# A retention and mixture-of-experts kernel: the first expert is chosen earlier, its register is read further back, low weight parts come in threes, and blocks of token rows are turned whole

## The chip, the cores and the metric

The kernel runs on one core of a Trainium2 chip. The core has five engines that run side by side, each with a queue of instructions that it works off in order: TensorE (PE in the profile, with its weight loads as PEld), VectorE (DVE), ScalarE (ACT), GpSimd (POOL) and SyncE (SP), which does little but issue transfers. A transfer can be issued from any queue; here SP loads inputs and weights, ACT stores token rows, and POOL fetches and stores rows by index. Engines wait for one another and for transfers by semaphores. The metric is the device time of one execution in microseconds (us).

## What is computed

A retention layer (attention without softmax, with a decay per head) makes 4608 token rows of 512 numbers. Each row with a positive skip score goes to the one of eight experts with the largest gate logit; the expert is two matrix products with a ReLU between them, and its result, times the gate's probability, is added to the row.

```python
scores = scale * np.matmul(q, k.transpose(0, 1, 3, 2))      # 8 x 8 heads, 576 x 576
Dmat = np.where(rel >= 0, gamma[:, None, None] ** rel[None, :, :], 0.0)
x = np.matmul(scores * Dmat, v)                             # as rows: 4608 x 512
...
do_compute = x @ w_skip > 0
e_idx = np.argmax(xc @ w_gate, axis=1)
gate_w = probs[np.arange(len(xc)), e_idx]
...
h = np.maximum(xc[mask] @ w1[e], 0.0)                       # 512 -> 1024
y[mask] = gate_w[mask, None] * (h @ w2[e])                  # 1024 -> 512
out[do_compute] = xc + y
```

## The kernel before

The program has two stages. In the **retention stage** a loop over g = 0 to 35 makes 128 token rows an iteration. The inputs of an iteration are one tile `u` of 1 MB, loaded from SP in two halves of 512 KB (`load_half`, L430-446) into five rotating buffers: the first half (queries and keys) can be issued when the tile of five iterations before has been read, the second (values and keys by row) is issued one iteration later, behind a block of products. In iteration g,

- GpSimd scales the keys of iteration g + 1 (`keys`, two instructions on L513, written `kn`). TensorE's state products of iteration g + 1 read them, and GpSimd reads the second half of `u`;
- TensorE interleaves the state products of chunk 2g (`ps_s`, L531) with the scores of the next iteration (`psc`, L479), then makes the values of iteration g - 1 (`pxt`, L560), then the second such pair of blocks, then turns the rows of iteration g - 2 (`px`, L584, in `stage_c`);
- ScalarE copies the running state back (L542) and stores token rows; VectorE applies the decays (L495) and evicts the values (L573).

**Gates.** Every fourth iteration logits are made (`pl`, `pn`), `route_a` turns them into masks on VectorE with one exponential on ScalarE (L155), and what is left of the routing stands in a list `todo`, from which `routing` takes a few entries an iteration: `route_b` (ranks of tokens in their experts), one `slots` entry for each group of 128 tokens (VectorE compares ranks to slot numbers, L228, tile `r`; TensorE adds the result to `ps_m`, L233, at the next call), and, after the first 24 groups, `choose_first`. That one counts the tokens of each expert so far, takes the largest as the first expert, and writes its number to `lead_id` (L261). `expert_reg` has SP load this number into a register, since every weight load takes its address from it. `close_first`, after 28 groups, makes the indices of the first expert's rows (`gi`, L295), which GpSimd fetches (L303).

**Weights.** Once the register is there, `weights()` is called at the end of each iteration. In call n it loads weight chunk n (512 KB, L130), and it splits chunk n - 2: ScalarE rounds it to a high part (L643), and GpSimd subtracts that from the chunk in four pieces, the low part (L648). Five chunks are split so in this stage.

In the **expert stage** TensorE runs through the eight experts. Rows of an expert are fetched in blocks of 128, 128 and what is left (`blocks`: for 368, 344, 332, 308, 304, 286, 278 and 276 slots that is 112, 88, 76, 52, 48, 30, 22 and 20 rows). `turn` transposes them 128 columns at a time, block by block (`pt`, L804), before the products of L387.

TensorE's queue is in the order in which the code is written (`manual_schedule`); on the other engines a scheduler orders the instructions by its own estimates, except that those given to `keep_in_program_order` keep their order among themselves. A pool's buffers rotate, and a writer waits for the last reader of its buffer.

In the list below, group 2 of the gates (`KONE`) is the one behind which the first expert is chosen, and its logits are routed in iteration 26.

```python
            if k == KONE:
                todo.append((True, 0, lambda: choose_first(ps_m, cnt)))
                todo.append((False, 0, lambda: regs.append(expert_reg(lead_id[0:1, 0:1]))))
```

An entry whose first field is True is only taken as the first of a call; the number is the iteration from which on it may be taken.

## Time and profile before

| what | us |
|---|---|
| median of 3 runs | 438.65 |
| the three runs | 432.28, 438.65, 443.81 |
| the profiled execution | 432.73 |
| its span, first to last instruction | 431.0 |
| TensorE busy in the span | 391.7 (91%) |
| VectorE, ScalarE, GpSimd busy | 276.3, 186.9, 160.4 |

The profile is of one execution that took 432.73 us, near the lower end of the runs. The page puts the span into 40 equal slices, one digit each, the busy share in tenths:

```profile
span 431.0 us, 13306 instructions
PE   7788988899988589999999999999999999999990
DVE  2595598488589978848755554865654755656430
POOL 4665564545555397150330042033141250400302
PEclk9899999999999989999999999999999999999996
DMA  8899989899986977255673455455465465642101
```

The slices are 10.8 us wide and counted from 0. Up to about 170 us (slice 15) is the retention stage: TensorE at eight or nine tenths, the transfers near full. From about 190 us on TensorE is full and the transfers are half used. Between them the first expert's products overlap with the last gates. In slice 13 TensorE falls to five tenths, and PEclk, the clock granted to it, falls in the slice behind.

### The profile page before, as it was taken

What the parts mean: (1) busy time and instruction counts of PE and PEld (TensorE: products, weight loads), DVE (VectorE), ACT (ScalarE), POOL (GpSimd) and SP (SyncE); (2) the same over time, 40 slices, a digit from 0 to 9 for tenths busy, and PEclk for the clock granted to TensorE, in tenths of its full rate; (3) what the DMA queues carried; (4) which work ended last, traced back from release to release, by engine and by line L of the source; (5) the groups of instructions that cost most, each with busy time, mean ns of one, the idle gap of its engine ahead of it and who ended that gap; (6) DMA issues with size and microseconds to landing.
All of it is one profiled execution on the core that took longest, in us unless ns stands there. A gap on an engine that the chain in (4) does not pass through costs nothing. (4 is left out here: it accounts for less than half of the span.)

```text
span 431.0 us, 13306 instructions
## 1 busy us (share of the span) xinstructions
PE 391.7 (91%) x5482; PEld 351.7 (82%) x5484; DVE 276.3 (64%) x562; ACT 186.9 (43%) x360; POOL 160.4 (37%) x182
## 2 busy tenths in 40 slices
PE   7788988899988589999999999999999999999990
PEld 3576776677777467888999999999999999999980
DVE  2595598488589978848755554865654755656430
ACT  2255444454644457117444434444444445445210
POOL 4665564545555397150330042033141250400302
PEclk9899999999999989999999999999999999999996
DMA  8899989899986977255673455455465465642101
GB/s 311 301 326 314 344 304 314 313 327 307 365 310 232 338 284 240 98 149 207 203 230 117 146 172 193 147 173 185 150 212 172 162 207 173 200 144 77 52 0 52
DMA packets 29023, 92.14 MB, mean 214 GB/s; under 512 B 4119, under 2 KB 4247, under 8 KB 28960
## 3 DMA queue, kind: packets, MB, share of 16 engines
q1 hardware_dynamic: 19584, 71.31, 48.4%
q0 software_dynamic: 3616, 9.86, 6.7%
q10 hardware_dynamic: 5760, 10.09, 6.3%
q8 instruction: 44, 0.72, 0.7%
q14 instruction: 19, 0.16, 0.1%
HBM read 77.07 MB, written 14.55 MB: 213 GB/s over the span
## 5 line engine op out<-in xcount | busy, mean ns | idle before, releaser
L140 DVE TENSOR_TENSOR wlo_w<-w,whi_w 128x1024 fp32r<-128x1024 f32 x59 | 71.9, 1223 | 61.9 <-ACT whi_w L139 61.8
L513 POOL TENSOR_TENSOR kn<-u,tt_sb 64x512 f32<-64x512 f32 x72 | 77.3, 1073 | 67.2 <-PE psc L479 44.2
L843 POOL DMA_INDIRECT out<-rs,sidx x24 | 32.8, 1366 | 156.4 <-DVE rs L842 153.2
L139 ACT CAST whi_w<-w 128x1024 fp32r<-128x1024 f32 x59 | 61.6, 1051 | 61.5 <-PE py L387 59.4
L542 ACT COPY u<-ps_s 64x256 f32<-64x256 f32 x128 | 47.0, 367 | 65.6 <-issue 26.7
L387 PE MATMUL py<-hhi,whi_w 128*128 128x344 f32 (+6 forms) x224 | 70.6, 315 | 0.0
L387 PE MATMUL ph<-xhi,whi_w 128*128 128x344 f32 (+6 forms) x224 | 68.9, 308 | 0.0
L387 PE MATMUL py<-hhi,wlo_w 128*128 128x344 f32 (+6 forms) x224 | 67.8, 303 | 0.0
L387 PE MATMUL ph<-xhi,wlo_w 128*128 128x344 f32 (+6 forms) x224 | 67.8, 302 | 0.0
L387 PE MATMUL ph<-xlo,whi_w 128*128 128x344 f32 (+6 forms) x224 | 67.7, 302 | 0.0
L387 PE MATMUL py<-hlo,whi_w 128*128 128x344 f32 (+6 forms) x224 | 67.6, 302 | 0.0
L531 PE MATMUL ps_s<-u,kn 64*64 64x64 f32 x1024 | 48.8, 227 | 14.4 <-issue 6.4
L531 PEld LDWEIGHTS ps_s<-u,kn 64*64 64x64 f32 x1024 | 39.2, 135 | 26.8 <-issue 10.8
L495 DVE TENSOR_TENSOR u<-psc,dt_sb 64x512 f32<-64x512 f32 x72 | 49.6, 689 | 14.2 <-PE psc L479 8.9
L395 ACT ACTIVATE hhi<-ph 128x344 fp32r<-128x344 f32 (+8 forms) x61 | 26.0, 427 | 64.1 <-PE ph L387 57.0
L479 PE MATMUL psc<-u 64*64 64x64 f32 x1152 | 51.8, 227 | 1.9 <-DVE u L495 0.6
L560 PE MATMUL pxt<-u 128*64 128x64 f32 x1152 | 45.1, 231 | 3.2 <-issue 2.8
L479 PEld LDWEIGHTS psc<-u 64*64 64x64 f32 x1152 | 41.7, 136 | 5.3 <-issue 2.4
L560 PEld LDWEIGHTS pxt<-u 128*64 128x64 f32 x1152 | 39.1, 142 | 7.5 <-issue 4.6
L387 PEld LDWEIGHTS py<-hhi,whi_w 128*128 128x128 f32 x224 | 42.2, 188 | 0.9
L387 PEld LDWEIGHTS ph<-xhi,whi_w 128*128 128x128 f32 x224 | 42.3, 189 | 0.1
L387 PEld LDWEIGHTS ph<-xlo,whi_w 128*128 128x128 f32 x224 | 42.3, 189 | 0.1
(178 smaller groups left out, 645.0 us busy)
## 6 DMA issues: line engine op xcount, KB each, us to landing
u<-qkv SPq DMA_DIRECT2D x72, 512.0 KB, 5.2
w<-w SPq DMA_DIRECT2D x64, 512.0 KB, 3.7
out<-xn ACTq DMA_DIRECT2D x36, 256.0 KB, 5.4
out<-rs,sidx POOLq DMA_INDIRECT x24
xg<-out,gidx POOLq DMA_INDIRECT x21
dt_sb<-dtab ACTq DMA_DIRECT2D x1, 256.0 KB
gt_sb<-dtab ACTq DMA_DIRECT2D x1, 256.0 KB
wg_sb<-wg ACTq DMA_DIRECT2D x1, 64.0 KB, 8.8
```

The source lines that it names most:

```text
L139: nc.scalar.copy(hi, t)
L140: nc.vector.tensor_tensor(lo, t, hi.bitcast(F32), ALU.subtract)
L387: nc.tensor.matmul(ps, x, y, start=first and n == 0, stop=last and n == 3 * len(terms) - 1)
L395: nc.scalar.activation(hi, ph, AF.Relu)
L479: nc.tensor.matmul(psc_t[g][halves[j], c, a, :], u[halves[j], 1 - j, c, a, :], u[halves[j], j, c, a, :], start=c == 0 and a == 0, stop=c = ...
L495: nc.vector.tensor_tensor(u_t[g][h, j], psc[halves[j]], dt_sb[h, c0 : c0 + 2], ALU.mult)
L513: nc.gpsimd.tensor_tensor(kn_t[g][h], u_t[g][h, 2 + j], tt_sb[h, 0, c0 : c0 + 2, :].unsqueeze(3).broadcast_to([D, 2, NPR, D]), ALU.mult,)
L531: nc.tensor.matmul(ps_s[halves[j], a, :], kn_t[g][h, c, a, :], u_t[g][h, 3 - j, c, a, :], start=n % NQ == 0 and a == 0, stop=a == NPR - 1, ...
L542: nc.scalar.copy(u_t[g][halves[j], 3 - j, c], ps_s[halves[j]])
L560: nc.tensor.matmul(pxt[halves[j], a, c * D : (c + 1) * D], u_t[g][:, 3 - j, c, a, :], u_t[g][:, j, c, a, :], start=c == 0 and a == 0, stop ...
L843: put = nc.gpsimd.indirect_dma_start(out=out, out_offset=bass.IndirectOffsetOnAxis(ap=sidx[:n, k, e : e + 1], axis=0), in_=rs[:n], in_offs ...
```

## The change

There are five edits, and the list of numbers is as before.

1. `choose_first` is put ahead of `route_b` in `todo`, from iteration 27 on, where it was behind it (iteration 29 in the code's order). The entries behind it move up: the first five slots of that group are added to `ps_m` in iteration 29 and not 31.
2. The register is no longer read by an entry of the list. The loop reads it behind the next second half of a `u` load (`issue_after`), and the `u` loads keep the order of the code; the first half of iteration g + 4 is now written behind the values of iteration g.
3. Low parts go into a list of pieces, of which `weights()` issues three a call; the rest follow behind the loop.
4. The keys keep their order against the pieces, once the register is there.
5. Blocks are fetched and turned as full 128 rows; the eviction reads only the columns that are used.

```diff
-            todo.append((False, g + 1 + (k <= KCUT), more))
             cnt = ra[4]
             if k == KONE:
-                todo.append((True, 0, lambda: choose_first(ps_m, cnt)))
-                todo.append((False, 0, lambda: regs.append(expert_reg(lead_id[0:1, 0:1]))))
+                todo.append((True, g + 1, lambda: chosen.append(choose_first(ps_m, cnt))))
+            todo.append((False, g + 1 + (k <= KCUT), more))
...
-            if g + UAHEAD < NT:
-                load_half(g + UAHEAD, 0)
+            if g == 0:
+                load_half(UAHEAD, 0)
...
-                load_half(g + UAHEAD - 1, 2, last_product())
+                half = load_half(g + UAHEAD - 1, 2, last_product())
+                if chosen and not regs:
+                    with tc.issue_after(half.ins):
+                        regs.append(expert_reg(lead_id[0:1, 0:1]))
...
                 values(2 * g - 1)
+                if g + UAHEAD < NT:
+                    load_half(g + UAHEAD, 0)
...
+        def low_parts(most):
+            for _ in range(min(most, len(pieces))):
+                tc.keep_in_program_order(nc.gpsimd.tensor_tensor(*pieces.pop(0), ALU.subtract))
...
                 for m in range(2):
                     for c in range(0, NCC, NCC // 2):
-                        some = lambda x: x[:, m, c : c + NCC // 2]
-                        tc.keep_in_program_order(
-                            nc.gpsimd.tensor_tensor(some(lo), some(t), some(hi).bitcast(F32), ALU.subtract)
-                        )
+                        pieces.append([x[:, m, c : c + NCC // 2] for x in (lo, t, hi.bitcast(F32))])
+            low_parts(3)
...
+                if regs:
+                    tc.keep_in_program_order(ins)
...
-            fetch(xg[:n, k, :], gidx[:n, k, e : e + 1])
+            fetch(xg[:, k, :], gidx[:, k, e : e + 1])
...
-                nc.tensor.transpose(
-                    pt[:, i, k * P - c0 : k * P - c0 + n], xg[:n, k, c * P : (c + 1) * P], ident[:n, :n]
-                )
+                nc.tensor.transpose(pt[:, i, k * P - c0 : (k + 1) * P - c0], xg[:, k, c * P : (c + 1) * P], ident)
```

Tiles carry a running number behind their name, which differs between the two programs: the `u` tiles of iterations 31 to 35 are 2300, 2373, 2467, 2571 and 2667 before and 2343, 2427, 2534, 2635 and 2727 now, and `kn` is the scaled keys made from the `u` that stands behind the arrow.

On GpSimd's queue near the end of the retention stage there stands before, from the clearing of iteration 31's state on:

```order
L525 MEMSET u_2300 64x256 x2
L513 TENSOR_TENSOR kn_2669<-u_2373,tt_sb 64x512 x2
L513 TENSOR_TENSOR kn_2760<-u_2467,tt_sb 64x512 x2
L648 TENSOR_TENSOR wlo_w_0_2569_2752<-w_0_2569,whi_w_0_2569_2751 128x256 x4
L513 TENSOR_TENSOR kn_2874<-u_2571,tt_sb 64x512 x2
L648 TENSOR_TENSOR wlo_w_1_2665_2866<-w_1_2665,whi_w_1_2665_2865 128x256 x4
L513 TENSOR_TENSOR kn_2991<-u_2667,tt_sb 64x512 x2
L303 DMA xg_130<-out,gi_2965 128x512 x2
```

and now on the same queue:

```order
L530 MEMSET u_2343 64x256 x2
L643 TENSOR_TENSOR wlo_w_0_2490_2689<-w_0_2490,whi_w_0_2490_2688 128x256 x3
L516 TENSOR_TENSOR kn_2696<-u_2427,tt_sb 64x512 x2
L643 TENSOR_TENSOR wlo_w_0_2490_2689<-w_0_2490,whi_w_0_2490_2688 128x256
L643 TENSOR_TENSOR wlo_w_1_2592_2769<-w_1_2592,whi_w_1_2592_2768 128x256 x2
L516 TENSOR_TENSOR kn_2776<-u_2534,tt_sb 64x512 x2
L643 TENSOR_TENSOR wlo_w_1_2592_2769<-w_1_2592,whi_w_1_2592_2768 128x256 x2
L643 TENSOR_TENSOR wlo_w_2_2694_2873<-w_2_2694,whi_w_2_2694_2872 128x256
L516 TENSOR_TENSOR kn_2880<-u_2635,tt_sb 64x512 x2
L303 DMA xg_130<-out,gi_2971 128x512 x2
L643 TENSOR_TENSOR wlo_w_2_2694_2873<-w_2_2694,whi_w_2_2694_2872 128x256 x3
L516 TENSOR_TENSOR kn_2994<-u_2727,tt_sb 64x512 x2
```

Three pieces now stand ahead of the keys of each of the iterations 32, 33 and 34, and the fetches and three pieces ahead of those of 35; before, the keys of 32 and 33 had none ahead of them, those of 34 and 35 four each, and no fetch.

On ScalarE's queue the first weight chunk is rounded behind the exponential of the gates that are routed in iteration 30; before:

```order
L155 ACTIVATE ex_2652<-ls_2650 128x32
L542 COPY u_2373<-ps_s 64x256 x2
L586 COPY xn_2727<-px_2722 128x512
L587 DMA out<-xn_2727 128x512
L643 CAST whi_w_0_2569_2751<-w_0_2569 128x1024
```

and now:

```order
L155 ACTIVATE ex_2675<-ls_2673 128x32
L654 CAST whi_w_0_2490_2688<-w_0_2490 128x1024
L591 COPY xn_2756<-px_2751 128x512
L592 DMA out<-xn_2756 128x512
L547 COPY u_2427<-ps_s 64x256 x2
```

The rounding has moved right behind the exponential, and the copies of the state that iteration 32 needs (`u_2373`, now `u_2427`) behind both.

On SP's queue there stands before, around the load of the register:

```order
L436 DMA u_2467<-qkv 128x1024
L321 TENSOR_LOAD lead_id
L130 ISA
L130 DMA w_0_2569<-w 128x1024
L436 DMA u_2571<-qkv 128x1024
L436 DMA u_2467<-qkv 128x1024
```

and now:

```order
L437 DMA u_2343<-qkv 128x1024 x2
L321 TENSOR_LOAD lead_id
L437 DMA u_2427<-qkv 128x1024
L130 ISA
L130 DMA w_0_2490<-w 128x1024
L437 DMA u_2427<-qkv 128x1024
```

The load of the register has moved from between the halves of iteration 33 to ahead of both halves of iteration 32, three half loads earlier in the queue.

More of the change, by code (lines that the diff above doesn't have):

```diff
@@ L350, in slot_ids @@
         nc.vector.tensor_scalar(gl, ids, float(-P), 0.0, ALU.add, ALU.max)
-        fetch(xg0[:n, k, :], gl[:n])
+        fetch(xg0[:, k, :], gl)
         raw = rt.tile([P, NBLK, NE, NCMP], F32, tag="raw", name="raw", bufs=1)
@@ L435, in load_half @@
                 u_t[g] = ap.tile([P, 4, 2, NPR, D], F32, tag="u", name=f"u_{g}", bufs=UBUFS)
-            half = nc.sync.dma_start(
-                u_t[g][:, s : s + 2].rearrange("p s c a i -> p (s c a i)"),
-                qkv[g, s // 2],
+            half = tc.keep_in_program_order(
+                nc.sync.dma_start(
+                    u_t[g][:, s : s + 2].rearrange("p s c a i -> p (s c a i)"),
+                    qkv[g, s // 2],
+                )
             )
@@ L446, in load_half @@
                 )
+            return half
         def load_u(g):
@@ L512, in keys @@
                 h = halves[1 - j]
-                nc.gpsimd.tensor_tensor(
+                ins = nc.gpsimd.tensor_tensor(
                     kn_t[g][h],
@@ L632 @@
         chunks = []
+        chosen = []
+        pieces = []
+        def low_parts(most):
+            for _ in range(min(most, len(pieces))):
+                tc.keep_in_program_order(nc.gpsimd.tensor_tensor(*pieces.pop(0), ALU.subtract))
         def weights():
@@ L734 @@
             weights()
+        low_parts(len(pieces))
         lt = logits_a(NT // NB - 1)
@@ L794, in gather @@
         for k, n in ks:
-            fetch(xg[:n, k, :], gidx[:n, k, e : e + 1])
+            fetch(xg[:, k, :], gidx[:, k, e : e + 1])
     def turn(e, xg, hi, lo, ks, cs, tag):
         c0, c1 = ks[0][0] * P, ks[-1][0] * P + ks[-1][1]
-        w = c1 - c0
+        w = len(ks) * P
         pt = bank(tag, f"pt_{e}_{cs[0]}_{c0}")[:, : len(cs) * w].rearrange("p (c i) -> p c i", i=w)
         for i, c in enumerate(cs):
-            for k, n in ks:
-                nc.tensor.transpose(
-                    pt[:, i, k * P - c0 : k * P - c0 + n], xg[:n, k, c * P : (c + 1) * P], ident[:n, :n]
-                )
-        split(hi[:, cs[0] : cs[-1] + 1, c0:c1], lo[:, cs[0] : cs[-1] + 1, c0:c1], pt)
+            for k, _ in ks:
+                nc.tensor.transpose(pt[:, i, k * P - c0 : (k + 1) * P - c0], xg[:, k, c * P : (c + 1) * P], ident)
+        split(hi[:, cs[0] : cs[-1] + 1, c0:c1], lo[:, cs[0] : cs[-1] + 1, c0:c1], pt[:, :, : c1 - c0])
     def down(e, f, ks, py, h, w):
```

## The prediction

> **What bounds the kernel now.** I read the busy time by stretches first, then what each engine waited for, then the order in time of SP, GpSimd, ScalarE, VectorE and TensorE from 125 to 175 us. By stretches (columns: TensorE, weight loads, VectorE, ScalarE, GpSimd busy, granted TensorE clock, share of the transfer engines, GB/s):
>
> ```profile
> 100.00:120.00 20.00, 18.23 (x506) 14.53 (x505) 13.70 (x23) 9.89 (x24) 11.14 (x13) 1.00 0.94 333
> ...
> 136.00:140.00 4.00, 4.00 (x128) 3.57 (x124) 3.74 (x11) 1.32 (x3) 2.10 (x2) 1.00 0.21 77
> ...
> 147.00:150.00 3.00, 0.14 (x9) 0.17 (x13) 2.85 (x6) 0.95 (x3) 2.93 (x4) 1.00 1.02 408
> 150.00:154.00 4.00, 3.94 (x99) 3.56 (x97) 3.90 (x6) 2.05 (x4) 3.85 (x5) 0.57 1.04 419
> ...
> 190.00:420.00 230.00, 229.31 (x1603) 221.62 (x1601) 135.50 (x220) 101.55 (x162) 50.30 (x38) 1.00 0.48 157
> ```
>
> Most of the retention stage runs on full transfers (0.94). From 190 us on TensorE is busy 229.31 of 230 us: what is saved on TensorE there is saved in the whole. In between, the transfers fall to 0.21, then TensorE does nothing for 3 us, then it has 0.57 of its clock. SP's queue tells the first:
>
> ```profile
> 126.03 5.41 SPq L436 DMA_DIRECT2D u<-qkv  x4
> 139.29 0.36 SPq L130 DMA_DIRECT2D w<-w  x1
> 139.87 0.81 SPq L436 DMA_DIRECT2D u<-qkv  x2
> ...
> SPq L321 <- DVE lead_id L261: 7.2, 1, 7.2
> ```
>
> After four loads, the last out at 131.44, SP stood at the register until VectorE had made the expert's number; the second half of iteration 33's inputs is the second of the two loads at 139.87, so it left past 140. GpSimd's queue shows who paid:
>
> ```profile
> 136.93 2.18 POOL L513 TENSOR_TENSOR kn<-u,tt_sb 64x512 f32<-64x512 f32 x2 [2.16 <-PE psc L479]
> 146.83 2.15 POOL L513 TENSOR_TENSOR kn<-u,tt_sb 64x512 f32<-64x512 f32 x2 [7.72 <-PE ps_m L188]
> 148.94 2.79 POOL L648 TENSOR_TENSOR wlo_w<-w,whi_w 128x256 fp32r<-128x256 f32 x4
> 151.81 2.29 POOL L513 TENSOR_TENSOR kn<-u,tt_sb 64x512 f32<-64x512 f32 x2
> ...
> 156.92 2.16 POOL L513 TENSOR_TENSOR kn<-u,tt_sb 64x512 f32<-64x512 f32 x2
> 159.26 1.26 POOL L303 DMA_INDIRECT xg<-out,gi  x1 [0.18 <-POOL kn L513]
> 160.83 1.00 POOL L303 DMA_INDIRECT xg<-out,gi  x1 [0.31 <-issue]
> ```
>
> These are the keys of iterations 32, 33, 34 and 35. Those of 33 waited 7.72 us; the profile names a product long done, but the landing of the late half is what came then. From there to the fetches GpSimd never rests: it is full with keys and low parts.
>
> VectorE is late too, and its order decides when the others go on:
>
> ```profile
> 131.94 2.95 DVE L228 TENSOR_SCALAR r<-iota,trank 128x384 bf16<-128x384 f16 x5
> 138.43 0.15 DVE L261 CAST lead_id<-top 128x1 int32<-128x1 f32 x1
> 140.64 0.31 DVE L608 TENSOR_REDUCE lg<-pn 128x36 f32<-128x144 f32 x1
> 144.81 0.77 DVE L228 TENSOR_SCALAR r<-iota,trank 128x384 bf16<-128x384 f16 x3
> 149.25 3.86 DVE L228 TENSOR_SCALAR r<-iota,trank 128x384 bf16<-128x384 f16 x4
> 155.25 0.17 DVE L246 SCALAR_TENSOR_TENSOR key<-ps_m,desc 128x8 f32<-128x8 f32 x1
> 157.19 0.80 DVE L295 TENSOR_SCALAR gi<-ids 128x2 int32<-128x2 f32 x1
> ...
> 141.43 0.23 ACT L155 ACTIVATE ex<-ls 128x32 f32<-128x32 f32 x1 [3.14 <-DVE ls L153]
> ...
> 163.37 0.23 ACT L155 ACTIVATE ex<-ls 128x32 f32<-128x32 f32 x1 [0.51 <-DVE ls L153]
> 163.50 1.03 ACT L643 CAST whi_w<-w 128x1024 fp32r<-128x1024 f32 x1
> ```
>
> Three comparisons take 0.77 us where GpSimd rests, four take 3.86 where it is full: the two block each other. ScalarE waited 3.14 us for the gates of iteration 30. On TensorE:
>
> ```profile
> 132.13 1.06 PE L592 MATMUL pl<-xt,wg_sb 128*32 128x512 f32 x8
> 149.86 0.24 PE L531 MATMUL ps_s<-u,kn 64*64 64x64 f32 x1 [3.16 <-ACT u L542]
> 161.56 0.68 PE L531 MATMUL ps_s<-u,kn 64*64 64x64 f32 x16 [0.60 <-issue]
> 166.61 0.98 PE L620 MATMUL pt_early<-ident,xg 128*128 128x128 f32 x7 [0.70 <-DMA xg<-out,gi]
> 169.58 0.48 PE L387 MATMUL ph_early<-x,whi_w 128*128 128x256 f32 x2
> ```
>
> Iteration 33 began at 149.86, 35 at 161.56, and the first expert's products at 169.58. That last time is what I follow for the retention stage.
>
> **Full blocks.** Starts of the products around a group of three transposes, with a last block of 76, 52 and 20 rows:
>
> ```profile
> 219.22 0.32 PE L387 MATMUL ph<-xlo,whi_w 128*128 128x344 f32 x1
> 219.37 0.32 PE L387 MATMUL ph<-xhi,wlo_w 128*128 128x344 f32 x1
> ...
> 220.02 0.32 PE L387 MATMUL py<-hlo,whi_w 128*128 128x344 f32 x1
> ...
> 251.85 0.32 PE L387 MATMUL ph<-xhi,wlo_w 128*128 128x332 f32 x1
> ...
> 252.76 0.32 PE L387 MATMUL py<-hlo,whi_w 128*128 128x332 f32 x1
> ...
> 373.92 0.29 PE L387 MATMUL ph<-xhi,wlo_w 128*128 128x278 f32 x1
> ...
> 374.75 0.29 PE L387 MATMUL py<-hlo,whi_w 128*128 128x278 f32 x1
> ```
>
> From the product before to the second behind it: 0.65, 0.91 and 0.83 us. Two product steps are in each (0.15 a step at 344 columns, 0.13 at 278 in proportion), which leaves 0.35, 0.61 and 0.57 us for three transposes. The smaller blocks cost more: a group whose last block has 64 rows or fewer seems to pay some 0.25 us that 76 rows do not. Five experts (52, 48, 30, 22, 20 rows) have four such groups each, 20 in all. A full block adds 52 columns to the 76-row case. They cost nothing at least, and at most what all 332 columns of that group cost on average, 0.35/332 = 1.05 ns each, 0.055 us. The transposes overlap in part, so I take 0.035, a little above the middle: 0.385 us a group against 0.59 on average, 20 x 0.205 = 4.1 saved. The groups with 88, 76 and 112 rows take on 4 x (40 + 52 + 16) columns at the same 0.67 ns, 0.3 more. Term: **-3.8 us**, from -4.8 (columns free) to -3.2. The fetches take some 576 more rows of 2 KB, 1.2 MB over a stage with the transfers at 0.48, an expert ahead: hidden, and if the cover went, 1.2 MB at 157 GB/s is 7.5 us spread over seven experts. The eviction reads what it read.
>
> **The register.** The number is made two iterations earlier (the row at 138.43 less 7 to 8 us, about 131). SP now stops for it behind the load that left at 126.03 and goes on at some 131.5, so four loads leave up to 4 us late, not 7. Iteration 32's second half lands at about 138 and its keys come later than that (below), so the 7.72 us wait goes, at no new price. Behind SP's wait only `u` loads and the first weight chunk are queued; a load takes some 6 us (out past 140, used at 146.83), so the chunk is there before ScalarE rounds it at 142. The first halves, now written behind the values, stand in SP's queue in the same turn as before and cost nothing; if one were late, its scores are three iterations off.
>
> **What is late next.** The five comparisons that stood at 131.94 now have their products in front of iteration 29's logits, so TensorE, which ran ahead, waits for them: with the six choosing instructions earlier in VectorE's queue they end about 0.8 later than 134.89, the logits begin near 136.2 and not at 132.13. VectorE itself was the later of the two: its reduction of the logits at 140.64 moves to about 141.0 (three more comparisons, 0.77, less their blocking). So the exponential is at 141.9, from 141.4 to 143. Now the chain, piece by piece:
> - rounding of chunk 0 starts 0.13 behind the exponential (163.37 to 163.50) and takes 1.03: done 143.1. Three pieces at 2.79/4: 145.2. Keys of 32 at 2.18: 147.4; before, 139.1.
> - three pieces and the keys of 33 (4.3 together): 151.7; before 148.98. Three pieces and the keys of 34: 156.0; before 154.1. The head start of before is eaten up by the pieces ahead of the keys.
> - iteration 33 begins at about 151.8 on TensorE (149.86 before). `gi` was ready at 157.99, 8.1 behind; the same would be 159.9. Two things may shorten it: the low clock of 150 to 154 is gone (1.7 lost, some 1.1 of it ahead of VectorE's 153.8), and GpSimd now waits while VectorE works from key to `gi`, which took 2.74 (eight instructions at key's 0.17 are 1.4, 1.3 less). That is 157.5 to 159.9; I take 158.9, nearer the upper end, since the comparisons ahead run beside a full GpSimd as they did.
> - GpSimd waits for `gi`, then fetches (2.57 from 159.26 to 161.83): 161.6; three pieces: 163.7; keys of 35: 165.9. State products of 35 begin at 166.1, before 161.56: +4.5.
> - From there to 169.58 it was 8.02 us, of which 0.70 was the wait for fetched rows; these are now in time: 7.3. TensorE then has rested for some 4 us ahead of 166, as it did at 147 to 150, and a stretch of the low clock follows: 0.9 of the 1.7 us that 150:154 lost (4.0 x 0.43), since some of it falls into waits for ScalarE.
>
> First expert's products at 174.3: **+4.7 us**. The last eight pieces follow the keys of 35, 5.6 us, to 171.5, and are needed by the fourth and fifth chunk's products, behind three chunks of early ones: hidden. One split of a whole chunk moves on VectorE from behind the turned rows to ahead of them; it costs nothing while VectorE waits for those rows, and 1.2 us at most:
>
> ```profile
> L140 DVE TENSOR_TENSOR wlo_w<-w,whi_w 128x1024 fp32r<-128x1024 f32 x59 | 71.9, 1223 | 61.9 <-ACT whi_w L139 61.8
> ```
>
> From below: the exponential at 141.4 and no wait for `gi` leave GpSimd's own queue, 1.2 + 3 x 4.3 + 2.6 + 2.1 + 2.2 + 0.3 = 21.3, so 162.7 and 170.0, +0.4. From above: the exponential at 143 (1.1), `gi` at 159.9 (1.0) and all of the low clock (0.8), +7.6.
>
> One choice in this chain can be weighed otherwise. The row from key to `gi`, 2.74 us, was measured beside a full GpSimd, and now GpSimd waits. The Trainium skill ("SBUF — State Buffer", Who interferes with whom) has the port pair that the two share as an exclusive lock, held for a whole instruction, with no other contention. By that rule alone nothing would block VectorE there, `gi` would come 1.3 earlier and the sum below would be -0.4, 438.2 us; by the rows I keep 158.9 and +0.9.
>
> **Sum.** -3.8 + 4.7 = +0.9 on the profiled execution's 432.73: 433.6. That execution lies 5.9 us below the median of the three runs, 438.65, to which the same step gives **439.5 us**.
>
> **Rivals.**
> - *Slower: the low clock comes at each wait for keys.* TensorE also rests ahead of iterations 30 and 32. If each such rest is as empty as 147:150 (0.14 busy of 3), two more stretches follow, 1.7 each: +3.4, 442.9 us. For it: the row 150:154. Against: there, GpSimd is the later one and hides TensorE's pace. It decides once the rest exceeds about 3 us. The Trainium skill ("TensorE: Matmul & The Clock Gate", Part 1) speaks for it: the clock halves after an idle window of about 3.4 us on a free-running grid; an estimate from that page is 1.7 us for each such window, as the rows have it.
> - *Faster: GpSimd's queue alone.* VectorE catches up, `gi` is never waited for: +0.4 - 3.8 = -3.4, 435.2 us. For it: 3.86 could shrink to 1.0. Against: GpSimd is full in just that place.
> - *The whole stall comes back.* If the pieces did not hold the keys, those of 33 would follow those of 32 after 5 us, as 34 follows 33 and 35 follows 34, and not after 9.9: -4.9, with the blocks -8.7, 430.0 us. Against: the order of GpSimd's queue.
> - *Full blocks do not help.* If the 0.25 us belongs to something else than the rows, 20 groups only pay their 76 to 108 columns, 0.06 each: +4.7 + 1.2 + 0.3 is 444.9 us. Against: 76 rows are not slow.
>
> **How the numbers follow.** My forecast 0.45, the low clock 0.2, GpSimd alone 0.22, the stall back 0.08, blocks without use 0.05. The likeliest gives 439.5. The runs shown scatter over 432.28 to 443.81, so each case is worth some 5 us either way; 430 to 446 leaves out about 2 in 10, and covers the bounds of the sum, -4.4 and +4.4 (434 to 443), with the scatter. A measurement of this kernel tells about 2% from no change, 8.8 us: faster by that is the half of "the stall back" and the low edge of "GpSimd alone", 0.11; slower is the upper edge of the low clock and of blocks without use, 0.08; within 2% 0.81.
>
> **What would show it.** Right: groups with a last block of 52 rows or fewer take 0.64 to 0.69 us and not 0.83 to 0.91, about 4 us off TensorE behind 190 us. SP waits under 5 us for `lead_id`. Keys of 32 end near 147 and those of 35 near 166, GpSimd waits for `gi`, first expert's products near 174. Wrong: keys of 32 before 143, or the first expert's products ahead of 169.

## The result, and the profile after

| | before | after |
|---|---|---|
| median, us (11 runs each) | 435.54 | 439.04 |
| lowest to highest, us | 430.16 to 443.81 | 435.45 to 441.36 |
| profiled execution, us | 432.73 | 440.37 |
| its span, us | 431.0 | 438.7 |
| its mean TensorE clock | 0.983 | 0.964 |

The ratio after to before is 1.0127, with a 95% interval of 1.008 to 1.0174: slower by about 1%, less than the 2% that the forecast counted as a change, and within the forecast's range. The further runs put the median of before at 435.5 instead of 438.65. Here and below the ratios leave out executions more than 1.5% above the fastest of their kernel (three took 909 to 1996 us) and the medians do not, so the two can differ by half a per cent (e12: its median over that of before in the same series is 0.994, its ratio 0.9989).

In what follows some lines have moved: the keys are L516 (L513 before), the low pieces L643 (L648), the rounding L654 (L643), the state copies L547 (L542), the state products L536 (L531), the logits L597 (L592). The experiments shift them by a few more.

The busy time by stretches after (TensorE, weight loads, VectorE, ScalarE, GpSimd busy, granted TensorE clock, share of the transfer engines, GB/s):

```profile
137.00:144.00 7.00, 6.68 (x115) 4.37 (x119) 4.44 (x12) 1.32 (x3) 0.62 (x2) 0.51 0.97 345
149.00:153.00 4.00, 0.00 (x0) 0.00 (x0) 3.84 (x7) 0.70 (x2) 3.78 (x5) 0.71 1.02 393
153.00:157.50 4.50, 4.37 (x97) 4.05 (x98) 1.02 (x3) 1.80 (x4) 3.17 (x4) 0.50 0.69 254
169.50:174.00 4.50, 0.00 (x0) 0.00 (x0) 4.27 (x8) 0.87 (x3) 3.75 (x6) 1.00 0.49 162
```

Where TensorE before had one empty stretch (147 to 150 us) and one at a low clock behind it, it now has two empty ones and a low clock in three places (the third, 174.5 to 178, below). SP's queue, what it waited for, in total, times, longest:

```profile
SPq L321 <- DVE lead_id L261: 4.2, 1, 4.2
```

That was 7.2. GpSimd in order of time (start, us, engine, line, operation, what ended the idle time ahead):

```profile
147.93 2.09 POOL L643 TENSOR_TENSOR wlo_w<-w,whi_w 128x256 fp32r<-128x256 f32 x3 [10.22 <-ACT whi_w L654]
150.09 2.16 POOL L516 TENSOR_TENSOR kn<-u,tt_sb 64x512 f32<-64x512 f32 x2
152.22 0.71 POOL L643 TENSOR_TENSOR wlo_w<-w,whi_w 128x256 fp32r<-128x256 f32 x1
154.17 1.41 POOL L643 TENSOR_TENSOR wlo_w<-w,whi_w 128x256 fp32r<-128x256 f32 x2 [1.24 <-ACT whi_w L654]
155.66 2.15 POOL L516 TENSOR_TENSOR kn<-u,tt_sb 64x512 f32<-64x512 f32 x2
...
160.75 0.73 POOL L643 TENSOR_TENSOR wlo_w<-w,whi_w 128x256 fp32r<-128x256 f32 x1 [1.57 <-PE pxt L565]
161.56 2.15 POOL L516 TENSOR_TENSOR kn<-u,tt_sb 64x512 f32<-64x512 f32 x2
165.75 1.23 POOL L303 DMA_INDIRECT xg<-out,gi  x1 [2.04 <-issue]
167.29 1.00 POOL L303 DMA_INDIRECT xg<-out,gi  x1 [0.31 <-issue]
168.31 2.09 POOL L643 TENSOR_TENSOR wlo_w<-w,whi_w 128x256 fp32r<-128x256 f32 x3
171.07 2.15 POOL L516 TENSOR_TENSOR kn<-u,tt_sb 64x512 f32<-64x512 f32 x2 [0.67 <-DMA xg<-out,gi]
```

The keys of 32 to 35 start at 150.1, 155.7, 161.6 and 171.1; before it was 136.9, 146.8, 151.8 and 156.9. The 7.72 us wait for a late half is gone, and GpSimd waits 10.22 us for ScalarE's rounding of chunk 0 instead, with the keys of 32 behind it. ScalarE:

```profile
146.63 0.23 ACT L155 ACTIVATE ex<-ls 128x32 f32<-128x32 f32 x1 [0.92 <-DVE ls L153]
146.77 1.03 ACT L654 CAST whi_w<-w 128x1024 fp32r<-128x1024 f32 x1
...
152.28 0.74 ACT L547 COPY u<-ps_s 64x256 f32<-64x256 f32 x2 [3.47 <-POOL kn L516]
153.05 1.04 ACT L654 CAST whi_w<-w 128x1024 fp32r<-128x1024 f32 x1
```

Chunk 0 is rounded right behind the exponential. Chunk 1 is rounded behind a state copy that had to wait for the keys of 32; its pieces stand ahead of the keys of 33. So a ring has closed: keys, state copy, rounding, pieces, next keys. TensorE:

```profile
137.16 1.46 PE L233 MATMUL ps_m<-mc,r 128*128 128x40 bf16 x15 [1.89 <-DVE r L228]
138.55 1.94 PE L597 MATMUL pl<-xt,wg_sb 128*32 128x512 f32 x8
...
153.13 0.33 PE L536 MATMUL ps_s<-u,kn 64*64 64x64 f32 x1 [4.71 <-POOL wlo_w L643]
...
174.10 0.77 PE L536 MATMUL ps_s<-u,kn 64*64 64x64 f32 x16 [4.65 <-POOL wlo_w L643]
...
182.12 0.50 PE L387 MATMUL ph_early<-x,whi_w 128*128 128x256 f32 x2
```

It waits 1.89 us for the moved slot comparisons in iteration 29, 4.71 ahead of 32 and 4.65 ahead of 35. The first expert's products start at 182.12 instead of 169.58. What is left of the span from there is 438.7 - 182.12 = 256.6 us, before 431.0 - 169.58 = 261.4: 4.8 less. The same groups of three transposes as in the prediction:

```profile
232.47 0.32 PE L387 MATMUL ph<-xhi,wlo_w 128*128 128x344 f32 x1
...
233.12 0.32 PE L387 MATMUL py<-hlo,whi_w 128*128 128x344 f32 x1
...
264.94 0.32 PE L387 MATMUL ph<-xhi,wlo_w 128*128 128x332 f32 x1
...
265.57 0.32 PE L387 MATMUL py<-hlo,whi_w 128*128 128x332 f32 x1
...
382.70 0.29 PE L387 MATMUL ph<-xhi,wlo_w 128*128 128x278 f32 x1
...
383.28 0.29 PE L387 MATMUL py<-hlo,whi_w 128*128 128x278 f32 x1
```

0.65 (76 rows then, 128 now), 0.63 (52 rows then: 0.91) and 0.58 us (20 rows then: 0.83). The 52 columns more of the first cost nothing that shows; the short blocks cost 0.25 to 0.28 a group. All twenty groups with a short last block read alike: 0.83 to 0.91 us before, 0.58 to 0.64 now, 5.3 us in sum.

### The profile page after: what moved, and what is told of

It is laid out like the page before. It is cut to its first block, busy times and chain, and to the rows that moved or that the text cites. A ratio compares the mean times of both kernels' runs of the same rounds, so it can differ in the third digit from the quotient of the medians.

```text
span 438.7 us, 13309 instructions
## 1 busy us (share of the span) xinstructions
PE 391.3 (89%) x5482; PEld 354.1 (81%) x5484; DVE 276.6 (63%) x562; ACT 185.8 (42%) x360; POOL 157.6 (36%) x182
## 4 chain that ended last, share of the span: by engine, by line
PE 41%; DMA 14%; issue 4%; POOL 2%; DVE 1%; ACT 0%; POOLq 0%; DVEq 0%; ACTq 0%
PE py L387 17%; PE ph L387 16%; DMA out<-rs,sidx 11%; PE pt L818 2%; PE yn L852 1%; DMA xg<-out,gidx 1%; PE ph_early L387 1%; DMA xg<-out,gl 1%; DMA xg<-out,gi 1%; PE ph L404 1%; POOL xg L303 1%; PE pxt L565 1%; POOL out L855 1%; PE px L589 0%; PE ph L405 0%
## 5 line engine op out<-in xcount | busy, mean ns | idle before, releaser
L516 POOL TENSOR_TENSOR kn<-u,tt_sb 64x512 f32<-64x512 f32 x72 | 76.7, 1065 | 61.5 <-PE psc L482 47.8
L855 POOL DMA_INDIRECT out<-rs,sidx x24 | 32.7, 1363 | 152.5 <-DVE rs L854 149.3
L547 ACT COPY u<-ps_s 64x256 f32<-64x256 f32 x128 | 46.9, 366 | 74.1 <-issue 29.5
L536 PEld LDWEIGHTS ps_s<-u,kn 64*64 64x64 f32 x1024 | 40.3, 140 | 36.5 <-issue 10.6
L536 PE MATMUL ps_s<-u,kn 64*64 64x64 f32 x1024 | 50.2, 232 | 21.9 <-POOL wlo_w L643 9.4
L498 DVE TENSOR_TENSOR u<-psc,dt_sb 64x512 f32<-64x512 f32 x72 | 49.6, 689 | 16.4 <-PE psc L482 12.6
L482 PE MATMUL psc<-u 64*64 64x64 f32 x1152 | 53.2, 231 | 2.2 <-issue 0.9
L565 PE MATMUL pxt<-u 128*64 128x64 f32 x1152 | 46.4, 236 | 3.9 <-issue 3.7
L482 PEld LDWEIGHTS psc<-u 64*64 64x64 f32 x1152 | 43.0, 141 | 5.7 <-issue 2.9
L578 DVE TENSOR_TENSOR xt<-pxt,gt_sb 128x512 f32<-128x512 f32 x36 | 24.8, 689 | 35.7 <-PE pxt L565 35.5
L565 PEld LDWEIGHTS pxt<-u 128*64 128x64 f32 x1152 | 40.5, 147 | 8.3 <-issue 5.6
```

The lines of the kernel that those rows point to most:

```text
L482: nc.tensor.matmul(psc_t[g][halves[j], c, a, :], u[halves[j], 1 - j, c, a, :], u[halves[j], j, c, a, :], start=c == 0 and a == 0, stop=c = ...
L498: nc.vector.tensor_tensor(u_t[g][h, j], psc[halves[j]], dt_sb[h, c0 : c0 + 2], ALU.mult)
L516: ins = nc.gpsimd.tensor_tensor(kn_t[g][h], u_t[g][h, 2 + j], tt_sb[h, 0, c0 : c0 + 2, :].unsqueeze(3).broadcast_to([D, 2, NPR, D]), ALU.mult,
L536: nc.tensor.matmul(ps_s[halves[j], a, :], kn_t[g][h, c, a, :], u_t[g][h, 3 - j, c, a, :], start=n % NQ == 0 and a == 0, stop=a == NPR - 1, ...
L547: nc.scalar.copy(u_t[g][halves[j], 3 - j, c], ps_s[halves[j]])
L565: nc.tensor.matmul(pxt[halves[j], a, c * D : (c + 1) * D], u_t[g][:, 3 - j, c, a, :], u_t[g][:, j, c, a, :], start=c == 0 and a == 0, stop ...
```

## The experiments

In each profile the retention stage comes to iteration 28 at another time, by up to 10 us: its first state product starts between 124.70 and 134.75. So the table gives the stretch from that product to the first expert's first product, when in it the keys of 35 start, and the mean clock granted to TensorE in it. Each stretch is that of one execution; that of e7 took 444.0 us, 5.7 more than its median. Ratios are to the kernel before, with 95% intervals.

| kernel | median, us | ratio | start of 28 | first product | stretch | keys of 35, in the stretch | clock in it |
|---|---|---|---|---|---|---|---|
| before | 435.5 | 1 | 124.70 | 169.58 | 44.9 | 32.2 | 0.96 |
| after | 439.0 | 1.0127 (1.008 to 1.0174) | 128.06 | 182.12 | 54.1 | 43.0 | 0.84 |
| e1 before, full blocks | 430.2 | 0.9878 (0.9836 to 0.992) | 127.47 | 170.78 | 43.3 | 31.1 | 0.92 |
| e2 after, old blocks | 445.2 | 1.0197 (1.0139 to 1.0255) | 129.72 | 183.46 | 53.7 | 41.7 | 0.84 |
| e3 after, keys free | 432.8 | 0.9943 (0.9908 to 0.9978) | 127.38 | 174.77 | 47.4 | 29.0 | 0.89 |
| e4 after, pieces late | 441.8 | 1.015 (1.0095 to 1.0205) | 128.81 | 184.44 | 55.6 | 40.1 | 0.82 |
| e5 after, keys of 35 first | 432.8 | 0.9943 (0.9893 to 0.9992) | 126.03 | 172.04 | 46.0 | 32.4 | 0.93 |
| e6 e4 + e5 | 433.9 | 0.9991 (0.9942 to 1.004) | 127.32 | 174.16 | 46.8 | 29.9 | 0.89 |
| e7 after, slots late | 438.3 | 1.0064 (1.0025 to 1.0103) | 134.75 | 186.25 | 51.5 | 39.8 | 0.87 |
| e8 e3 + e7 | 431.2 | 0.9969 (0.9911 to 1.0027) | 126.10 | 170.46 | 44.4 | 27.7 | 0.92 |
| e9 e5 + e7 | 432.1 | 0.9942 (0.9895 to 0.9989) | 125.14 | 172.80 | 47.7 | 33.0 | 0.89 |
| e10 e6 + e7 | 435.7 | 0.9999 (0.9962 to 1.0035) | 128.69 | 177.42 | 48.7 | 28.7 | 0.86 |
| e11 e10, five chunk buffers | 433.8 | 0.9966 (0.993 to 1.0003) | 126.87 | 172.87 | 46.0 | 28.7 | 0.93 |
| e12 e1, register behind 33 | 432.5 | 0.9989 (0.9921 to 1.0058) | 129.16 | 172.97 | 43.8 | 29.5 | 0.92 |

**The full blocks, alone and taken away.** e1 is the kernel before with them, e2 the changed kernel without them (the reverse of this diff, and of the like in `gather` and for the last block of the first expert):

```diff
-                nc.tensor.transpose(
-                    pt[:, i, k * P - c0 : k * P - c0 + n], xg[:n, k, c * P : (c + 1) * P], ident[:n, :n]
-                )
+                nc.tensor.transpose(pt[:, i, k * P - c0 : (k + 1) * P - c0], xg[:, k, c * P : (c + 1) * P], ident)
```

> The kernel before with the full 128-row blocks alone. Theory (the blocks are worth what the traces of before and after show: 20 groups of three transposes whose last block has 20 to 52 rows go from 0.84-0.92 to 0.59-0.63 us, 0.26 us each): about 5 us less than before, 430.3 against 435.5 (ratio 0.986 to 0.990), and the retention stage as before, the first expert's first product at 169 to 171 us. Rival 1 (the blocks are worth the 3.8 us of the prediction at most, part of the gain being given back at the hidden-layer copies): 431.7 to 432.5. Rival 2 (TensorE's shorter groups only turn into waits for VectorE's splits): 435.5, ratio 1.000.

> The changed kernel with the blocks as they were (last blocks of 20 to 112 rows turned and fetched short), everything else of the change kept. Theory (two separate terms, blocks -5 and retention stage +8 to +9): 5 us above the changed kernel, 444.3 (ratio to before about 1.020), the first expert's first product where the changed kernel has it, 180 to 182 us. Rival (the early choice is worth nothing or little, and the blocks nothing): 439, ratio 1.008.

Measured: 430.2 and 445.2. The blocks take 4.8 us off the kernel before (434.96 in that series) and 6.1 off the changed one (439.04 in its own), and the rest of the change costs about as much with them as without (8.9 us and 10.2). Spans less first products: e1 428.3 - 170.78 = 257.5 against 261.4, e2 444.7 - 183.46 = 261.2 against 256.6: 3.9 and 4.6 us. The rivals by which the blocks are worth nothing fall. The one by which a part is given back does not: in e1's profile TensorE waits 1.27 us at 195.95 for VectorE at the hidden layer (`part`, L410), a wait that the profile of before does not have, and the interval's upper end, 0.992, reaches that rival's 0.991. The blocks alone have the lowest median of this study; the intervals of e3, e5, e8 and e9 overlap with theirs.

**Which part of the row on GpSimd costs.** e3 leaves the keys to the scheduler again. e4 keeps them in order, but issues the pieces in fours from two calls later. e5 writes the keys of 35 in iteration 33, ahead of the fetches, and changes nothing else. e6 is e4 and e5 together:

```diff
-                if regs:
-                    tc.keep_in_program_order(ins)
```

```diff
-            low_parts(3)
+            low_parts(4 if n >= 4 else 0)
```

```diff
-            if ahead:
+            if ahead and g < NT - 2:
                 keys(g + 1)
...
+            if g == NT - 3:
+                keys(NT - 1)
             if lt is None:
                 routing(0 if g == NT - 1 else 3 if g < starts[KCUT + 1] else 8)
```

> The changed kernel with the keys' products free of the written order again: the scheduler then puts the keys of 32 ahead of chunk 0's four low pieces on GpSimd, the keys of 33 ahead of chunk 1's, and the keys of 35 ahead of chunk 2's. Theory (keys stand behind pieces that wait for the late rounding, and TensorE stands for 4.7 us each ahead of iterations 32 and 35): the keys of 32 start at 139 to 142 us instead of 150.1, TensorE's 4.7 us ahead of iteration 32 go, and the keys of 33 still wait for chunk 0's pieces (start 151 to 153 instead of 155.7); the time falls by 3 to 6 us against the changed kernel, to 433 to 436 (ratio to before 0.994 to 1.002). Rival 1 (SyncE's stop and the late loads hold the keys, whatever the order): keys of 33 and on where they were, time 438 to 440. Rival 2 (TensorE's wait for the slot comparisons and the low clock behind it cost the time): 437 to 439.

> The changed kernel with the low pieces in fours from two calls later: the keys of 32 and 33 ahead of every piece, chunk 0's pieces between the keys of 33 and 34, chunk 1's between the keys of 34 (and the fetches) and of 35, chunk 2's and the rest behind the keys of 35. Theory: the keys start when their halves have landed, 32 at about 139 to 140, 33 at about 146, 34 at about 150 to 152, 35 at about 160 to 162; state products of 35 begin at about 162 to 164 instead of 174.1, and the first expert's first product at 171 to 173 instead of 182; time 429 to 432 (ratio to before 0.985 to 0.992). Rival 1 (SyncE's stop is the cause): the halves land late, the keys with them, 437 to 440. Rival 2 (TensorE's wait at iteration 29 and the clock): 436 to 439. Rival 3 (the weight chunks become the bound: chunk 4's load waits for chunk 0's pieces, and its rounding stands on ScalarE in front of the retention's last copies): the state products are early but the first expert's products still start at 178 or later, 436 or more.

> The changed kernel with one thing moved: the keys of 35 are written ahead of the two fetches of the first expert's rows and the three low pieces behind them (in the changed kernel they stand behind both, where TensorE stands 4.65 us ahead of iteration 35); keys of 32 to 34 behind their pieces as in the changed kernel. Theory (the last place in the row decides, since what an earlier held-up key costs is partly waited for at the next one): the keys of 35 start at about 164 instead of 171.1, the wait ahead of iteration 35 goes, state products of 35 at about 169.5 instead of 174.1; 4 to 5 us less than the changed kernel, 434 to 435 (ratio to before 0.997 to 1.001). Rival 1 (each held-up key costs for itself, the wait of 4.7 us ahead of iteration 32 as much as the one ahead of 35): 436 to 437. Rival 2 (the fetches come later instead, and the turned rows of the first expert wait): 438 to 439.

> The kernel of the experiment with late pieces, with the keys of 35 written ahead of the fetches as well: keys of 32, 33, 35 ahead of every fetch and of all but chunk 0's pieces. Theory (in the run with late pieces the whole gain at 32 to 34 was waited away at 35: TensorE stood 7.27 us ahead of iteration 35, its keys behind fetches that waited for gi until 163.5 and four pieces): that wait goes, state products of 35 at 164.7 to 166 instead of 171.9, 6 to 7 us less than 441.8, 434.5 to 436 (ratio to before 0.999 to 1.003), and near the run with free keys (432.8). Rival 1 (the loads of the weights bound it): 439 to 441. Rival 2 (more is won, since GpSimd no longer holds TensorE at all): 430 to 432.

e3 fell to 432.8, a little below what was expected; e5, at 432.8, and e6, at 433.9, came out below their ranges too, by 1.2 and 0.6. e4 was a miss: no piece held the keys of 32 and 33 any more, those of 34 stood behind four pieces that waited for nothing, and the time rose. GpSimd and TensorE in e4:

```profile
148.15 2.15 POOL L516 TENSOR_TENSOR kn<-u,tt_sb 64x512 f32<-64x512 f32 x2 [1.68 <-PE px L589]
150.27 2.77 POOL L643 TENSOR_TENSOR wlo_w<-w,whi_w 128x256 fp32r<-128x256 f32 x4
153.11 2.18 POOL L516 TENSOR_TENSOR kn<-u,tt_sb 64x512 f32<-64x512 f32 x2
163.49 1.23 POOL L303 DMA_INDIRECT xg<-out,gi  x1 [8.20 <-issue]
165.03 1.00 POOL L303 DMA_INDIRECT xg<-out,gi  x1 [0.30 <-issue]
166.06 2.75 POOL L643 TENSOR_TENSOR wlo_w<-w,whi_w 128x256 fp32r<-128x256 f32 x4
168.89 2.15 POOL L516 TENSOR_TENSOR kn<-u,tt_sb 64x512 f32<-64x512 f32 x2
```

```profile
171.91 1.12 PE L536 MATMUL ps_s<-u,kn 64*64 64x64 f32 x16 [7.27 <-POOL wlo_w L643]
```

The keys of 34 were done at 155.3. Then GpSimd stood 8.20 us in front of the first fetch, which needs `gi`, and the keys of 35 stood behind it (their inputs were there: the last load of the stage left at 149.3, and none took more than 7.6 us), behind the second fetch and four pieces. What was won at 32 to 34 was waited away there. e5 moves only those keys:

```profile
156.19 4.43 POOL L516 TENSOR_TENSOR kn<-u,tt_sb 64x512 f32<-64x512 f32 x4
161.59 1.23 POOL L303 DMA_INDIRECT xg<-out,gi  x1 [0.97 <-POOL kn L516]
```

```profile
164.01 0.68 PE L536 MATMUL ps_s<-u,kn 64*64 64x64 f32 x16
...
172.04 0.51 PE L387 MATMUL ph_early<-x,whi_w 128*128 128x256 f32 x2 [0.59 <-DVE x L145]
```

The four instructions are the keys of 34 and 35 in one go. TensorE does not wait ahead of 35, and the kernel falls from 439.0 to 432.8, although it still waits 3.42 us ahead of iteration 32. So the place of the keys of 35 behind the fetches and pieces is worth about 6 us by the medians, and 7.9 where it is changed alone once more (e4 to e6, 441.8 to 433.9); the wait ahead of 32 is worth little by itself. The stretches say somewhat more than the move does: 3.1 of the 8.1 us by which e5's is shorter lie in iteration 29, whose code is the same (9.0 us in the profile of after, 5.9 in e5's); from the start of iteration 30 to the first product it is 41.7 and 36.5. In the table, the four kernels whose keys of 35 start 39.8 us or more into the stretch (after, e2, e4, e7) are the four slow ones. Three of them, after, e2 and e4, also have the lowest clock: in the rows of 149 to 157.5 and of 169.5 to 178 half the clock followed where a wait for keys had left TensorE empty, so these 6 us are the wait and the clock behind it together.

**The slot comparisons in iteration 29.** e7 gives the slots of that group a due time two iterations later; e8 and e9 add this to e3 and e5:

```diff
-                todo.append((False, 0, lambda t=t: slots(t)))
+                todo.append((False, g + 3 if k == KONE else 0, lambda t=t: slots(t)))
```

> The changed kernel with the first five slot comparisons and their slot additions two iterations later (31 instead of 29, where the kernel before has them); first expert, register, pieces and keys as changed. Theory of the prediction's chain (five comparisons in iteration 29 make TensorE wait 1.89 us, half clock follows from 137 to 143.8, the exponential and with it chunk 0's rounding come late, and with that the pieces and the keys of 32): the wait at 29 goes, the exponential ends at 141 to 143 instead of 146.6, the keys of 32 start at 145 to 146 instead of 150.1; but the keys of 35 still stand behind the fetches, so at most 1 to 2 us less than the changed kernel, 437 to 438.5 (ratio 1.003 to 1.010). Rival 1 (this wait and the clock are the main cause of the +8 us in the retention stage): 431 to 434. Rival 2 (the comparisons only wait elsewhere, gi comes later by as much): 439 to 441.

> The kernel with the keys free again (432.8), with the slot comparisons and additions at iteration 31 as well. What is left between it and the blocks alone (430.2) is then the moved choice, the register and the thirds. Theory (the wait of 1.57 us at iteration 29 and the half clock behind it are what is left): 430 to 431.5. Rival 1 (the comparisons meet GpSimd's pieces later and wait 2 us there, as in that run at iteration 33): 432.5 to 434. Rival 2 (SyncE's stop at the register costs the rest): 432 to 433.

> The kernel with the keys of 35 ahead of the fetches (432.8), and the first five slot comparisons and additions at iteration 31 as well. Theory (the two terms add up: the slot comparisons in iteration 29 cost 2 to 3 us, seen as 7.3 to 9.0 us from the start of iteration 29 to that of 30 in every run that has them there and 4.2 to 4.8 in every run that has not): from the first state product of 28 to the first expert's first product 43 to 44 us instead of 46.0, time 429.5 to 431 (ratio to before about 0.988). Rival 1 (the comparisons are paid later, where they meet the low pieces at iterations 31 to 33): 432 to 434.

e7 came out at 438.3, as expected; its ratio of 1.0064 and that of after, 1.0127, have intervals that overlap. Iteration 29 falls from 9.0 us (131.40 to 140.41) to 4.8 (138.09 to 142.89). But e8 is 431.2 against 432.8 with overlapping intervals, and e9 is where e5 was: the expected 2 to 3 us did not add up. The rule that they rested on, 7.3 us or more in every run with the comparisons in iteration 29, does not hold for e5 itself, with 5.9. In e9 TensorE waits 4.75 us ahead of iteration 32 where e5 waited 3.42. In this pair of profiles, what iteration 29 gives, the next wait for keys takes.

**Trying to beat the blocks alone.** e10 adds the late slots to e6, e11 a fifth buffer for the weight chunks to that. e12 takes the late half of 33 out of e1 by reading the register behind both halves of 33, without the early choice, the thirds and the order of the keys; of the change it has only the blocks and the written order of the `u` loads:

```diff
-        t = wpool.tile([P, 2, NCC, P], F32, tag="w", name=f"w_{e}_{f}", bufs=4)
+        t = wpool.tile([P, 2, NCC, P], F32, tag="w", name=f"w_{e}_{f}", bufs=5)
```

```diff
-                todo.append((True, 0, lambda: choose_first(ps_m, cnt)))
-                todo.append((False, 0, lambda: regs.append(expert_reg(lead_id[0:1, 0:1]))))
+                todo.append((True, 0, lambda: last_half.append(choose_first(ps_m, cnt))))
...
                 load_half(g + UAHEAD - 1, 2, last_product())
+                if len(last_half) > 1 and not regs:
+                    with tc.issue_after(last_half[0].ins):
+                        regs.append(expert_reg(lead_id[0:1, 0:1]))
```

(`last_half[0]` is the load written last.)

> The kernel with late pieces and the keys of 35 ahead of the fetches (433.9), and the slot comparisons at iteration 31 as well. Theory (terms add up): 2 to 3 us less, 431 to 432; the 11.1 us from the state products of 35 to the first expert's first product stay, since chunk 5's load still waits for chunk 1's pieces, and ScalarE's copies behind its rounding. Rival 1 (GpSimd free of pieces while the comparisons run makes them cheap, 0.25 to 0.5 us each): 428 to 430. Rival 2 (comparisons paid elsewhere): 434.

> The kernel of the run before with five buffers for the weight chunks instead of four, so that chunk 5's load waits for no low piece of chunk 1 (chunk 4's for none of chunk 0). Theory: the load of chunk 5 goes out before 160 us, ScalarE's wait of 3.0 us for it goes, and the stretch from the state products of 35 to the first expert's first product falls from 11.1 to about 8 us: 428 to 429.5 (ratio about 0.984 to 0.987), under the blocks alone (430.2). Rival (the first product waits for GpSimd's late pieces or the fetched rows instead): 431 to 432, as the run before.

> The kernel before with the full blocks, the first expert chosen where it was, and the register read behind both halves of 33 instead of between them (the loads in the changed kernel's written order; the weight chunks one iteration later, with that chunk 0's pieces between the keys of 34 and 35 instead of between 33 and 34). It takes away the late half of 33 without the early choice and without pieces ahead of the keys. Theory (the 7 us wait of the keys of 33 cost TensorE 2.55 us ahead of iteration 33 in the run with the blocks alone, and a stretch of half clock behind it): the keys of 33 start at about 143 instead of 148.5, 2 to 3 us less than the blocks alone, 427.5 to 428.5 (ratio to before 0.980 to 0.984). Rival 1 (the place of that wait is not what decides, since gi and the fetches hold the end of the stage; as with the wait of 4.7 us ahead of iteration 32 in the changed kernel, whose removal gained nothing by itself): 429.5 to 431. Rival 2 (the later chunks cost: a chunk's load waits for the late pieces and ScalarE for it, as in the runs with late pieces): 432 to 435.

All three missed: 435.7, 433.8 and 432.5. In e10 TensorE still waited 1.98 us for the keys of 32, 1.77 in iteration 32 for VectorE and 1.84 ahead of 35. In e11 the stretch from the state products of 35 to the first products did fall, to 8.25 us (164.62 to 172.87), as expected, but from 9.4 in e10 and not from the 11.1 of e6; the time fell by 1.9 against e10, and waits of 1.60, 1.65 and 1.11 us stayed at the same three places. In e12 GpSimd had the keys of 33 early:

```profile
143.90 2.15 POOL L517 TENSOR_TENSOR kn<-u,tt_sb 64x512 f32<-64x512 f32 x2 [1.19 <-PE ps_s L535]
151.02 2.32 POOL L517 TENSOR_TENSOR kn<-u,tt_sb 64x512 f32<-64x512 f32 x2 [4.97 <-PE psc L483]
```

But SP stood 4.0 us for `lead_id` in front of the halves of 34, and the keys of 34 waited 4.97 us instead. The stop went one iteration on. The stretch, 43.8, is that of e1, 43.3; 432.5 lies in the range of the second rival, later chunks, and the runs do not tell its cost from that of the moved stop.

## Why the prediction was right, and where it was not

The forecast, 439.5 us, and the measured 439.0 agree better than its steps do, and so close an agreement is luck. The forecast put +0.9 on the three runs' median of 438.65, which lies 3.1 above that of eleven; the change is +3.5 on 435.54. The two terms were -3.8 and +4.7; by the profiles they are -4.8 and +9.2.

- **Full blocks.** Right, and a little under: -3.8 forecast, -4.8 by the spans behind the first product, the end of the range given for columns that cost nothing. A group was taken at 0.385 us for its transposes; 0.63 less two steps of 0.15 is 0.33. e1 and e2 show the term by itself, at 3.9 to 6.1 us by spans and medians. That a last block pays up to 64 rows is not measured: it pays at 52 and does not at 76.
- **The register.** SP's wait is 4.2 us, under the 5 given, and the 7.72 us wait is gone, as forecast. "At no new price" held, but no run shows a gain from its removal either: e12 and e8 are without it, and their stretches, 43.8 and 44.4, are those of e1 and of before. Neither is a clean test: in e12 the keys of 34 wait in its place, and e8 has the early choice and the thirds.
- **What is late next.** The mechanism was right in its order: TensorE waits for the moved comparisons, the exponential is late, chunk 0's rounding behind it holds the pieces and these the keys, and the keys of 35 come last, behind the fetches. The term was mis-sized, +4.7 for 54.1 - 44.9 = +9.2. On the forecast's own path, counted from the first state product of iteration 28 (forecast less 124.70, measured less 128.06):

| | forecast | measured | later by |
|---|---|---|---|
| exponential | 17.2 | 18.6 | 1.4 |
| keys of 33 done | 27.0 | 29.8 | 2.8 |
| iteration 33 begins on TensorE | 27.1 | 30.6 | 3.5 |
| `gi` ready | 34.2 | 36.8 | 2.6 |
| keys of 35 done | 41.2 | 45.2 | 4.0 |
| state products of 35 | 41.4 | 46.0 | 4.6 |
| first expert's products | 49.6 | 54.1 | 4.5 |

- The exponential: the logits began no later than foreseen (10.5 us into the stretch, 11.5 forecast), but then TensorE ran at half clock, 1.94 us for 1.06 in the logits alone. The forecast took VectorE for the later of the two; it waited 2.51 us for TensorE's values (the first line below).
- The step whose mechanism was wrong is "three pieces and the keys of 33 (4.3 together)". The keys of 33 and 34 followed at 5.57 and 5.90 us (150.09, 155.66, 161.56), since the pieces between them waited 1.24 and 1.57 us for the roundings of chunks 1 and 2. The forecast had only chunk 0's rounding in the chain and took GpSimd to be full; the roundings stand behind state copies that wait for the keys, the ring described above. On the path this is 1.3 us, at the keys of 33; what those of 34 lost was not paid again, since GpSimd then stood 2.04 us for `gi`.
- From the end of the keys to the state products that read them it is 0.88 us each time (157.81 to 158.69, 173.22 to 174.10). The forecast put 0.1 and 0.2, though the rows of before show the same 0.88 (148.98 to 149.86): 1.5 us together.
- From the key to `gi` the forecast stayed near the row of before, 2.74 us, though GpSimd would wait. It took 1.15 (163.66 to 164.81), and from the start of iteration 33 to `gi` it was 6.1 and not 7.1. The rule of the Trainium skill weighed there ("SBUF — State Buffer", Who interferes with whom) was the better guide in that place. Behind it, the fetch began 0.94 after `gi`, and the keys waited 0.67 more behind the pieces; from `gi` to the end of the keys of 35 it was 8.4 instead of 7.0.

```profile
143.50 0.69 DVE L578 TENSOR_TENSOR xt<-pxt,gt_sb 128x512 f32<-128x512 f32 x1 [2.51 <-PE pxt L565]
...
163.66 0.17 DVE L246 SCALAR_TENSOR_TENSOR key<-ps_m,desc 128x8 f32<-128x8 f32 x1
...
164.64 0.17 DVE L295 TENSOR_SCALAR gi<-ids 128x2 int32<-128x2 f32 x1
```

- From the state products of 35 to the first products: 8.2 forecast, 8.0 measured, with the low clock in it.
- **Rivals.** GpSimd's queue alone (435.2) fell, since GpSimd did wait for `gi`. The whole stall coming back (430.0) did not come about, since the pieces did hold the keys; e8 and e12, where no late half holds the keys of 33, are not below the blocks alone, so neither shows the 4.9 us. Blocks without use fell with e1. The low clock did come at three places, and not one, as the slower rival had it. Its price was not measured by itself, since e3, e8 and e9 differ from their partners in waits too. An upper bound can be worked out: TensorE is busy for 14.35 us of its half-clock windows after (137.1 to 143.8, 150.7 to 157.5, 174.5 to 178) and for 3.34 us before (150.5 to 153.9), and full clock would take half of that away. The difference, an estimate, is at most some 5.5 of the 9.2 us; how much of it falls into waits stays open.

What the runs leave open: e5 is 2.6 us above e1, and their intervals (0.9893 to 0.9992, 0.9836 to 0.992) overlap. Whether the early choice, the register and the thirds cost anything beyond the place of the keys of 35 can't be told. The two parts of the profiles, +9.2 and -4.8, make +4.4 where the medians show +3.5; a stretch is of one execution, and iteration 29 alone differs by 3.1 us between two executions with the same code there.

## What to carry to other kernels

When work is pinned into one order on an engine, follow the queue to its last item that the critical engine needs: here an instruction that waited for an index stood ahead of the last keys, and 6 us hung on that one place, while freeing the earlier keys gained nothing (after to e4, e5 to e6). Removing a wait upstream pays only if nothing downstream waits for something else; moving the stop for a register by one iteration moved the stall by one iteration. And before costing a chain at its engine's rates, look for a ring: if an item's input is made behind that item's own consumer, the spacing is the ring's length, not the engine's time.

## What was not expected of the hardware

Less the two product steps, three transposes took 0.32 to 0.35 us whether the last block had 76 or 128 rows, and 0.57 to 0.61 when it had 52 or 20.

TensorE's clock fell without an empty stretch. Windows of 3.4 us after (columns as above):

```profile
133.70:137.10 3.40, 1.57 (x49) 1.20 (x43) 3.26 (x7) 1.32 (x3) 2.14 (x3) 0.99 0.53 166
137.10:140.50 3.40, 3.18 (x27) 1.11 (x31) 3.35 (x10) 0.00 (x0) 0.56 (x2) 0.50 0.86 266
...
174.50:178.00 3.50, 3.50 (x50) 2.93 (x47) 3.34 (x6) 1.56 (x4) 3.50 (x7) 0.51 0.38 113
```

A window that was busy for 1.57 of 3.4 us, with no rest longer than 1.89, was followed by half the clock, as the empty ones were; and the window behind it, busy for 3.18 us, was followed by half the clock again (0.50 from 140.5 to 143.8). The Trainium skill ("TensorE: Matmul & The Clock Gate", Part 1) ties the low clock to an idle window of about 3.4 us; the length agrees with these rows, that the window must be idle does not.

Beside a busy GpSimd, one VectorE instruction took longer than any single one of GpSimd's. In e3:

```profile
148.50 1.00 DVE L205 CAST cp<-gt 128x4 bf16<-128x4 f32 x1
149.53 0.17 DVE L206 TENSOR_TENSOR gt<-gt,cp 128x4 f32<-128x4 f32 x1
149.74 2.96 DVE L207 CAST cp<-gt 128x4 bf16<-128x4 f32 x1
```

A cast of four numbers a row took 2.96 us, while GpSimd ended the keys of 33 (at 150.6, about 1.1 us for each of the two) and ran three pieces of 0.70 us (from 150.57 on). That GpSimd is what held it is read from the overlap; no run tests it.
